# A second expert layer by quarters with seven block products in place of eight, in a fused attention and expert kernel

## The chip, the cores and the metric

One core of a Trainium2 chip runs the whole program. The metric is device microseconds of one execution, as a median of several runs on one chip. Executions of one kernel mostly lie within about 0.3% of each other, so a difference of 1 or 2 us is not read from a total here, but from the traces.

Engine names are those of the profile: PE is TensorE, PEld its weight loads, DVE VectorE, ACT ScalarE, POOL GpSimd, SP SyncE. L432 is line 432 of the kernel that the profile is of; line numbers move from one kernel to the next. The granted clock is the share of its full clock that TensorE was given, as the trace records it.

## The reference

```python
# q, k, v: (8 batches, 8 heads, 576, 64); 4 experts; w1: (4, 512, 1024), w2: (4, 1024, 512)
k_p, v_p = k and v averaged over groups of 8 positions        # 72 keys and values
attn = softmax(q @ k_p.T / 8);  x = attn @ v_p                 # 4608 tokens of 512
p = domain_probs / (domain_probs.sum(-1) + 1e-9)
for e in range(4):
    h = relu(x @ w1[e])
    out += p[:, e] * (h @ w2[e])          # the second expert layer
```

## The kernel before

Tokens come in nine chunks of 512: eight from one batch each, and one of what the batches leave over. Four experts make 36 pairs of chunk and expert. In step s, TensorE does the first layer of pair s and, in turns with it, the second layer of pair s-1. Pieces of the next chunk's attention are strewn into the four steps of a chunk. The order on each engine is fixed by the program. A bank is a part of PSUM, the memory that takes TensorE's results; an evacuation is the instruction of VectorE (DVE) or ScalarE (ACT) that reads a result out of its bank; a fold is VectorE's averaging of one batch's keys or values over groups of 8. The remainder is the ninth chunk.

```python
psum_a = tile_pool(bufs=2)   # attention: two pairs of banks
psum_h = tile_pool(bufs=2)   # first layer: two banks
psum_o = tile_pool(bufs=2)   # second layer: two banks
...
def down(c, e, r):                      # second layer, 128 tokens
    o_ps = psum_o.tile([P, DM], F32)
    for fc in range(8):
        matmul(o_ps, lhsT=H_sb[:, fc, r*P:(r+1)*P], rhs=w2_bf[:, e, fc, :])   # 128x512
    if e == 0: nc.scalar.activation(out=acc[:, r, :], in_=o_ps, func=Copy, scale=prob)
    else:      nc.vector.scalar_tensor_tensor(acc[:, r, :] = o_ps * prob + acc[:, r, :])
...
def scores(b, pair):                    # 64 rows: pairs, which start 3 to 4 ns apart in the trace
    matmul(sc_ps[0:72, r2, hh], lhsT=kpT[lo:lo+64, h, 0:72], rhs=qT[lo:lo+64, h])   # x4
    nc.scalar.activation(out=expT, in_=sc_ps[0:72], func=Exp)
...
for i in range(4):                      # one step
    up(c, e, two of the eight fc); slot(); down(previous pair, i); slot()
```

The softmax here doesn't subtract the row's maximum and nothing guards it: scores larger than these inputs give would overflow.

## Time and profile before

| | before |
|---|---|
| median of runs | 555.96 us |
| PE busy, granted clock | 543.2 us (98%), 0.999 |
| DVE busy, ACT busy | 28%, 42% |
| start to start, 128x512 matmul with its own weights | 216 ns |

The first view is the page of the kernel before: busy time and count of instructions of each engine, and the chain that ended last.

```profile
PE 543.2 (98%) x2975; PEld 251.5 (45%) x2975; DVE 154.0 (28%) x254; ACT 233.3 (42%) x375; POOL 40.3 (7%) x59
...
PE 90%; DMA 8%; POOL 1%; DVE 0%; issue 0%; ACT 0%; POOLq 0%
```

TensorE is the bound, and the chain of waits runs through it. The groups of the same page say what it does. Columns: line, engine, operation, output and inputs, sizes, count; then busy time and mean ns of one; then idle time before.

```profile
L432 PE MATMUL o_ps<-w_bf,H_sb 128*128 128x512 bf16 x1152 | 271.7, 379 | 0.0
L443 DVE SCALAR_TENSOR_TENSOR acc<-o_ps,p_all,acc 128x512 f32<-128x512 f32 x108 | 81.1, 751 | 331.6 <-PE o_ps L432 331.2
```

The mean of 379 ns is the duration that the trace gives one matmul (its end is modelled); as one starts every 216 ns, the records overlap. What a matmul costs is read from start to start. The next view is the timeline of PE (start us, duration us, engine, line, group):

```profile
32.90 1.89 PE L432 MATMUL o_ps<-w_bf,H_sb 128*128 128x512 bf16 x8
34.63 1.89 PE L422 MATMUL h_ps<-xT,w_bf 128*128 128x512 bf16 x8
...
219.61 0.41 PE L243 MATMUL sc_ps<-qT,kpT 64*72 64x256 bf16 x4
219.95 1.90 PE L432 MATMUL o_ps<-w_bf,H_sb 128*128 128x512 bf16 x8
```

Eight matmuls of 512 columns take 34.63 - 32.90 = 1.73 us, 216 ns each. A step has 64 of them, 13.82 us, and a step without attention takes 13.81 us in the trace: nothing else is left in it. In the first steps TensorE waits for a load, in the same view (in brackets the idle time before the first of the group, and what ended it):

```profile
47.76 0.40 PE L228 MATMUL qt_ps<-ident,q_sb 128*128 128x128 bf16 x4 [0.88 <-DMA q_sb<-in_q_dram]
```

### The profile page before, as it was taken

What the parts mean: (1) busy time and instruction counts of PE and PEld (TensorE: products, weight loads), DVE (VectorE), ACT (ScalarE), POOL (GpSimd) and SP (SyncE); (2) the same over time, 40 slices, a digit from 0 to 9 for tenths busy, and PEclk for the clock granted to TensorE, in tenths of its full rate; (3) what the DMA queues carried; (4) which work ended last, traced back from release to release, by engine and by line L of the source; (5) the groups of instructions that cost most, each with busy time, mean ns of one, the idle gap of its engine ahead of it and who ended that gap; (6) DMA issues with size and microseconds to landing.
All of it is one profiled execution on the core that took longest, in us unless ns stands there. A gap on an engine that the chain in (4) does not pass through costs nothing.

```text
span 553.9 us, 7058 instructions
## 1 busy us (share of the span) xinstructions
PE 543.2 (98%) x2975; PEld 251.5 (45%) x2975; DVE 154.0 (28%) x254; ACT 233.3 (42%) x375; POOL 40.3 (7%) x59
## 2 busy tenths in 40 slices
PE   8899999999999999999999999999999999999996
PEld 4654444444444444444444444444444444444442
DVE  2404435033502342132403250335023201220122
ACT  1653533633364335533463346333643344334330
POOL 6410301000020002000200020000000000000000
PEclk9999999999999999999999999999999999999999
DMA  9999996900591139302851178004001110011003
GB/s 125 209 208 206 200 91 141 132 20 19 108 142 16 28 80 156 49 20 39 161 66 28 11 153 120 20 19 108 20 11 29 54 33 0 2 47 39 0 1 76
DMA packets 73407, 41.37 MB, mean 75 GB/s; under 512 B 44688, under 2 KB 67216, under 8 KB 73376
## 3 DMA queue, kind: packets, MB, share of 16 engines
q0 software_dynamic: 32032, 22.63, 28.2%
q1 hardware_dynamic: 41344, 18.29, 15.3%
q8 instruction: 23, 0.38, 0.3%
q14 instruction: 8, 0.07, 0.1%
HBM read 45.16 MB, written 9.44 MB: 99 GB/s over the span
## 4 chain that ended last, share of the span: by engine, by line
PE 90%; DMA 8%; POOL 1%; DVE 0%; issue 0%; ACT 0%; POOLq 0%
PE o_ps L432 44%; PE h_ps L422 42%; DMA q_sb<-in_q_dram 5%; DMA w_bf<-in_moe_w_dram 2%; PE sc_ps L243 2%; PE c_ps L268 1%; DMA x_rem<-x_tok 0%; POOL kraw L84 0%; PE scr_ps L306 0%; POOL q_sb L92 0%; POOL vraw L84 0%; DVE acc L443 0%; PE c_ps L322 0%; PE qt_ps L228 0%; ACT expT L246 0%
## 5 line engine op out<-in xcount | busy, mean ns | idle before, releaser
L426 ACT ACTIVATE H_sb<-h_ps 128x512 bf16<-128x512 f32 (+1 forms) x296 | 173.2, 585 | 249.6 <-PE h_ps L422 247.7
L432 PE MATMUL o_ps<-w_bf,H_sb 128*128 128x512 bf16 x1152 | 271.7, 379 | 0.0
L422 PE MATMUL h_ps<-xT,w_bf 128*128 128x512 bf16 (+1 forms) x1056 | 242.8, 373 | 0.8 <-ACT xT L286 0.4
L443 DVE SCALAR_TENSOR_TENSOR acc<-o_ps,p_all,acc 128x512 f32<-128x512 f32 x108 | 81.1, 751 | 331.6 <-PE o_ps L432 331.2
L422 PEld LDWEIGHTS <-w_bf 128*128 128x128 bf16 x1184 | 113.0, 98 | 130.1 <-issue 4.9
L432 PEld LDWEIGHTS <-H_sb 128*128 128x128 bf16 x1152 | 110.2, 98 | 131.1 <-issue 2.7
L440 ACT ACTIVATE acc<-o_ps,p_all 128x512 f32<-128x512 f32 x36 | 24.7, 687 | 39.4 <-PE o_ps L432 39.4
L246 ACT ACTIVATE expT<-sc_ps 72x1024 bf16<-72x1024 f32 x32 | 32.0, 1011 | 3.6 <-PE sc_ps L243 3.6
L422 PE MATMUL h_ps<-x_rem,w_bf 128*128 128x512 bf16 x128 | 30.2, 379 | 0.2 <-DMA x_rem<-x_tok 0.2
L257 DVE TENSOR_TENSOR x_tok<-c_ps,inv 128x512 bf16<-128x512 f32 x36 | 24.9, 692 | 1.2
L398 POOL COPY gate<-kpT 1x1 bf16<-1x1 bf16 x6 | 2.1, 348 | 264.8 <-DMA kpT<-kp_97 144.8
L268 PEld LDWEIGHTS <-expT 72*128 72x128 bf16 x256 | 12.4, 98 | 7.8 <-ACT expT L246 0.9
L256 DVE RECIPROCAL inv<-c_ps 128x8 f32<-128x8 f32 x36 | 7.3, 203 | 26.2 <-PE c_ps L268 17.2
L157 DVE TENSOR_TENSOR kraw<-kraw 72x2048 bf16<-72x2048 bf16 x7 | 8.5, 1212 | 20.7 <-DMA kraw<-in_k_dram 20.7
L243 PE MATMUL sc_ps<-qT,kpT 64*72 64x256 bf16 x128 | 13.1, 282 | 0.6 <-ACT expT L246 0.5
L205 PE MATMUL w_ps<-zeros 128*128 128x512 bf16 x31 | 10.8, 488 | 1.2 <-DVE zeros L459 1.2
L243 PEld LDWEIGHTS <-kpT 64*72 64x72 bf16 x128 | 4.8, 107 | 12.9 <-issue 12.3
L157 DVE TENSOR_TENSOR vraw<-vraw 72x2048 bf16<-72x2048 bf16 x7 | 8.5, 1210 | 0.0
L92 POOL DMA_DIRECT2D q_sb<-in_q_dram x9 | 7.8, 870 | 2.0 <-issue 2.0
L84 POOL DMA_DIRECT2D kraw<-in_k_dram x9 | 7.6, 843 | 2.4 <-PE xt_ps L285 2.0
L84 POOL DMA_DIRECT2D vraw<-in_v_dram x9 | 7.3, 810 | 1.5 <-issue 0.5
L102 POOL DMA_DIRECT2D q_rem<-in_q_dram x8 | 5.6, 698 | 8.4 <-DMA w_bf<-in_moe_w_dram 8.4
(56 smaller groups left out, 88.0 us busy)
## 6 DMA issues: line engine op xcount, KB each, us to landing
out_dram<-acc SPq DMA_DIRECT2D x32, 256.0 KB, 2.4
w_bf<-in_moe_w_dram POOLq DMA_DIRECT2D x7, 1024.0 KB, 23.1
kraw<-in_k_dram POOLq DMA_DIRECT2D x7, 576.0 KB, 11.2
vraw<-in_v_dram POOLq DMA_DIRECT2D x7, 576.0 KB, 13.7
q_sb<-in_q_dram POOLq DMA_DIRECT2D x7, 512.0 KB, 7.0
w_bf<-in_moe_w_dram POOLq DMA_DIRECT2D x2, 512.0 KB, 12.6
out_dram<-acc SPq DMA_DIRECT2D x8, 128.0 KB, 2.3
kraw<-in_k_dram POOLq DMA_DIRECT2D x2, 288.0 KB, 5.3
```

The costliest lines, as they stand in the source:

```text
L84: nc.gpsimd.dma_start(out=raw[:, hs], in_=src[b, hs].rearrange("h (j r) d -> j h r d", r=POOL))
L157: nc.vector.tensor_add(out=raw[:, hs, 0:4, :], in0=raw[:, hs, 0:4, :], in1=raw[:, hs, 4:8, :])
L205: nc.tensor.matmul(w_ps[:], lhsT=zeros[:, 0:P], rhs=zeros[:])
L243: nc.tensor.matmul(sc_ps[0:SP, r2, hh], lhsT=kpT[lo:lo + D, h, 0:SP], rhs=qT[lo:lo + D, h])
L246: nc.scalar.activation(out=expT[:, 2 * pair:2 * pair + 2].rearrange("j h a b t -> j b (h a) t"), in_=sc_ps[0:SP].rearrange("j b h a t -> j ...
L257: nc.vector.tensor_tensor(out=x_tok[:], in0=c[:, :, :, 0:D], in1=inv[:].unsqueeze(3).to_broadcast([P, 2, NPAIR, D]), op=ALU.mult,)
L268: nc.tensor.matmul(c_ps[:, h // NPAIR, at:at + D + 1], lhsT=expT[:, h, r // 2, r % 2, :], rhs=vp[:, h, :],)
L422: nc.tensor.matmul(out_ps, lhsT=w1_bf[:, e, kc, fc * P:(fc + 1) * P], rhs=xT[:, kc, at], start=(kc == 0), stop=(kc == KC - 1),)
L426: nc.scalar.activation(out=H_sb[:, fc, at], in_=out_ps, func=ACT.Relu)
L432: nc.tensor.matmul(o_ps[:], lhsT=H_sb[:, fc, r * P:(r + 1) * P], rhs=w2_bf[:, e, fc, :], start=(fc == 0), stop=(fc == FCH - 1),)
L440: nc.scalar.activation(out=accs[c][:, r, :], in_=o_ps[:], func=ACT.Copy, scale=prob)
L443: nc.vector.scalar_tensor_tensor(out=dst, in0=o_ps[:], scalar=prob, in1=dst, op0=ALU.mult, op1=ALU.add,)
```

## The change

A block product of 2 by 2 quarters needs eight products of quarters. A known scheme (Winograd's form of Strassen's) gets by with seven, for eight sums of quarters. Here the quarters of the hidden layer are `a11..a22` (halves of the tokens by halves of the hidden columns), those of the weights `b11..b22`. Sums of weights are made once for each expert, sums of hidden quarters in each step, all in bf16 on VectorE. The scheme shares partial results: a bank is read by VectorE as soon as one product is in it, goes on growing by the next product, and is read again for another quarter of the output.

```diff
-    psum_a bufs=2; psum_o bufs=2; accpool bufs=2; hpool bufs=3
+    psum_a bufs=1; psum_o: four banks o0..o3; one acc; hpool bufs=2
...
+    def weight_sums(e):                       # once for each expert, in place for b12
+        t0 = b12 - b11;  b12 = b22 - b12;  t1 = b22 - t0;  t2 = b21 - t1
+    early_sum: S3 = a11 - a21;  hidden_sums: S1 = a21 + a22, S2 = S1 - a11;  last_sum: S4 = a12 - S2
...
+        chain, grows, lhs, rhs, row, col, first = [
+            ("o0", 0, a11, b11, 0, 0, True),  ("o2", 0, a12, b21, 0, 0, False),
+            ("o0", 1, S2, t1, 0, 1, True),    ("o2", 0, S1, t0, 1, 1, True),
+            ("o0", 1, S3, b12, 1, 1, False),  ("o2", 1, S4, b22, 0, 1, False),
+            ("o0", 1, a22, t2, 1, 0, True)][step]
+        for j in range(2):                    # two banks of 128 tokens x 256 columns
+            for i in range(4):
+                matmul(o_ps, lhsT=lhs[:, i, j*P:(j+1)*P], rhs=rhs[:, i, :],
+                       start=(not grows and i == 0), ...)
+            if e == 0 and first: nc.scalar.activation(out=dst, in_=o_ps, func=Copy, scale=prob)
+            else: nc.vector.scalar_tensor_tensor(dst = o_ps * prob + dst)
...
-                lhsT=kpT[lo:lo + D, h, 0:SP]
+                lhsT=key_columns(b, h, lo)    # 128 columns, 56 of them not used
...
+            if (s, i) in ((0, 6), (1, 5), (3, 0), (3, 6)): weight_sums(...)   # experts 1 to 4
```

A step then has 32 matmuls of 512 columns for the first layer and 56 of 256 for the second. The first batch's attention borrows product banks, since they are free at that time.

More of the change, by code (lines that the diff above doesn't have):

```diff
@@ L51 @@
     rawpool = ctx.enter_context(tc.tile_pool(name="rawpool", bufs=1))
-    apool = ctx.enter_context(tc.tile_pool(name="apool", bufs=2))
+    apool = ctx.enter_context(tc.tile_pool(name="apool", bufs=1))
     xpool = ctx.enter_context(tc.tile_pool(name="xpool", bufs=2))
     npool = ctx.enter_context(tc.tile_pool(name="npool", bufs=2))
-    hpool = ctx.enter_context(tc.tile_pool(name="hpool", bufs=3))
-    accpool = ctx.enter_context(tc.tile_pool(name="accpool", bufs=2))
-    psum_a = ctx.enter_context(tc.tile_pool(name="psum_a", bufs=2, space=bass.MemoryType.PSUM))
+    hpool = ctx.enter_context(tc.tile_pool(name="hpool", bufs=2))
+    spool = ctx.enter_context(tc.tile_pool(name="spool", bufs=1))
+    psum_a = ctx.enter_context(tc.tile_pool(name="psum_a", bufs=1, space=bass.MemoryType.PSUM))
     psum_h = ctx.enter_context(tc.tile_pool(name="psum_h", bufs=2, space=bass.MemoryType.PSUM))
-    psum_o = ctx.enter_context(tc.tile_pool(name="psum_o", bufs=2, space=bass.MemoryType.PSUM))
+    psum_o = ctx.enter_context(tc.tile_pool(name="psum_o", bufs=1, space=bass.MemoryType.PSUM))
     w1_bf = wpool.tile([P, E, KC, F], BF16, name="w1_bf")
     w2_bf = wpool.tile([P, E, FCH, DM], BF16, name="w2_bf")
+    wt_bf = wpool.tile([P, E, 3, FCH // 2, DM // 2], BF16, name="wt_bf")
+    acc = const.tile([P, NR, DM], F32, name="acc")
     x_rem = const.tile([P, NPAIR, NT], BF16, name="x_rem")
@@ L70 @@
     kps = [const.tile([SPT, H, 2, D], BF16, name=f"kp{i}") for i in range(2)]
+    kpTs = [const.tile([P, H + 1, SPT], BF16, name=f"kpT{i}") for i in range(3)]
     vps = [const.tile([SP, H, D + 1], BF16, name=f"vp{i}") for i in range(3)]
@@ L154, with spare_bank @@
     state = {}
+    turns = [0]
+    def spare_bank():
+        turns[0] += 1
+        return psum_o.tile([P, NT], F32, tag=f"o{turns[0] % 4}", name="spare")
     def fold(raw, hs):
@@ L170, in keys @@
     def keys(b, hs):
-        if hs.start == 0:
-            state[("kpT", b)] = apool.tile([P, H, SPT], BF16, name="kpT", bufs=3)
+        state[("kpT", b)] = kpTs[b % 3]
         if b >= BUSY:
             nc.sync.dma_start_transpose(
-                out=state[("kpT", b)][:], in_=kps[b % 2][:].rearrange("j h a d -> j (h a d)")
+                out=state[("kpT", b)][:, 0:H], in_=kps[b % 2][:].rearrange("j h a d -> j (h a d)")
             )
             return
-        kpt_ps = psum_o.tile([P, H, SP], BF16, tag="o_ps", name="kpt_ps")
+        kpt_ps = one_bank(b).bitcast(BF16)[:, 0:H * SP].rearrange("p (h j) -> p h j", j=SP)
         for h in range(hs.start, hs.stop):
@@ L223, in queries @@
             return
-        pool, tag = (psum_o, "o_ps") if b == 0 else (psum_a, "a")
-        qt_ps = pool.tile([P, 2, 2, P], BF16, tag=tag, name="qt_ps")
+        qt_ps = one_bank(b).bitcast(BF16)[:, 0:4 * P].rearrange("p (h a t) -> p h a t", h=2, a=2)
         for hh in range(2):
@@ L230, in queries, with key_columns @@
                 )
-        nc.vector.tensor_copy(out=state[("qT", b)][:, 2 * pair:2 * pair + 2], in_=qt_ps[:])
+        nc.vector.tensor_copy(out=state[("qT", b)][:, 2 * pair:2 * pair + 2], in_=qt_ps)
+    def key_columns(b, h, lo):
+        return state[("kpT", b)][:].rearrange("p h j -> p (h j)")[lo:lo + D, h * SPT:h * SPT + P]
     def scores(b, pair):
-        kpT, qT = state[("kpT", b)], state[("qT", b)]
+        qT = state[("qT", b)]
         if pair == 0:
@@ L237, in scores @@
         expT = state[("expT", b)]
-        sc_ps = psum_a.tile([P, 2, 2, 2, P], F32, tag="a", name="sc_ps")
+        banks = two_banks(b == 0 and pair % 2)
         for hh in range(2):
@@ L243, in scores, with one_bank, two_banks, whole @@
                 nc.tensor.matmul(
-                    sc_ps[0:SP, r2, hh], lhsT=kpT[lo:lo + D, h, 0:SP], rhs=qT[lo:lo + D, h]
-                )
-        nc.scalar.activation(
-            out=expT[:, 2 * pair:2 * pair + 2].rearrange("j h a b t -> j b (h a) t"),
-            in_=sc_ps[0:SP].rearrange("j b h a t -> j b (h a) t"),
-            func=ACT.Exp, scale=EXP_SCALE,
-        )
-    def divide(c_ps, x_tok):
-        c = c_ps[:, :, 0:NPAIR * (D + 1)].rearrange("p a (h d) -> p a h d", d=D + 1)
-        inv = npool.tile([P, 2, NPAIR], F32, name="inv")
-        nc.vector.reciprocal(out=inv[:], in_=c[:, :, :, D])
-        nc.vector.tensor_tensor(
-            out=x_tok[:], in0=c[:, :, :, 0:D],
-            in1=inv[:].unsqueeze(3).to_broadcast([P, 2, NPAIR, D]), op=ALU.mult,
-        )
+                    banks[r2][:, hh * 2 * P:(hh + 1) * 2 * P],
+                    lhsT=key_columns(b, h, lo), rhs=qT[lo:lo + D, h],
+                )
+        exp_out = expT[:, 2 * pair:2 * pair + 2].rearrange("j h a b t -> j b (h a) t")
+        for sc, r2 in whole(banks):
+            nc.scalar.activation(
+                out=exp_out[:, r2], in_=sc[0:SP].rearrange("j b (g t) -> j b g t", t=P),
+                func=ACT.Exp, scale=EXP_SCALE,
+            )
+    def one_bank(b):
+        return spare_bank()[:] if b == 0 else two_banks(False)[0]
+    def two_banks(spare):
+        if spare:
+            return [spare_bank()[:], spare_bank()[:]]
+        t = psum_a.tile([P, 2, NT], F32, tag="a", name="a_ps")
+        return [t[:, 0], t[:, 1], t]
+    def whole(banks):
+        if len(banks) == 3:
+            return [(banks[2][:], slice(0, 2))]
+        return [(banks[i].unsqueeze(1), slice(i, i + 1)) for i in range(2)]
+    def divide(banks, x_tok):
+        for ps, hs in whole(banks):
+            n = hs.stop - hs.start
+            c = ps[:, :, 0:NPAIR * (D + 1)].rearrange("p a (h d) -> p a h d", d=D + 1)
+            inv = npool.tile([P, 2, NPAIR], F32, name="inv")
+            nc.vector.reciprocal(out=inv[:, 0:n], in_=c[:, :, :, D])
+            nc.vector.tensor_tensor(
+                out=x_tok[:, hs], in0=c[:, :, :, 0:D],
+                in1=inv[:, 0:n].unsqueeze(3).to_broadcast([P, n, NPAIR, D]), op=ALU.mult,
+            )
     def context(b, r):
@@ L264, in context @@
         x_tok = npool.tile([P, 2, NPAIR, D], BF16, name="x_tok", bufs=4)
-        c_ps = psum_a.tile([P, 2, NT], F32, tag="a", name="c_ps")
+        banks = two_banks(b == 0 and r % 2)
         for h in range(H):
@@ L268, in context @@
             nc.tensor.matmul(
-                c_ps[:, h // NPAIR, at:at + D + 1],
+                banks[h // NPAIR][:, at:at + D + 1],
                 lhsT=expT[:, h, r // 2, r % 2, :], rhs=vp[:, h, :],
             )
-        divide(c_ps, x_tok)
+        divide(banks, x_tok)
         state[("x", b, r)] = x_tok
@@ L282, in turn @@
             return
-        xt_ps = psum_o.tile([P, KC, P], BF16, tag="o_ps", name="xt_ps")
+        xt_ps = spare_bank()[:].bitcast(BF16)[:, 0:KC * P].rearrange("p (k t) -> p k t", t=P)
         for kc in range(KC):
             nc.tensor.transpose(xt_ps[:, kc, :], x_tok[:, kc * P:(kc + 1) * P], ident[:])
-        nc.scalar.copy(out=dst, in_=xt_ps[:])
+        nc.scalar.copy(out=dst, in_=xt_ps)
     def rem_queries(i):
@@ L301, in rem_scores @@
         for bb in range(2):
-            kpT = state[("kpT", 2 * i + bb)]
             for pair in range(NPAIR):
@@ L306, in rem_scores @@
                     nc.tensor.matmul(
-                        scr_ps[0:SP, hh, bb, pair, :],
-                        lhsT=kpT[lo:lo + D, 2 * pair + hh, 0:SP],
+                        scr_ps[:, hh, bb, pair, :],
+                        lhsT=key_columns(2 * i + bb, 2 * pair + hh, lo),
                         rhs=qTr[lo:lo + D, pair, bb, :],
@@ L317, in rem_context @@
         x_tok = npool.tile([P, 2, NPAIR, D], BF16, name="x_tok", bufs=4)
-        c_ps = psum_a.tile([P, 2, NT], F32, tag="a", name="c_ps")
+        banks = two_banks(False)
         for h in range(H):
@@ L322, in rem_context @@
                 nc.tensor.matmul(
-                    c_ps[bb * REM:(bb + 1) * REM, h // NPAIR, at:at + D + 1],
+                    banks[h // NPAIR][bb * REM:(bb + 1) * REM, at:at + D + 1],
                     lhsT=expTr[:, h % 2, bb, h // 2, :], rhs=vps[(2 * i + bb) % 3][:, h, :],
                 )
-        divide(c_ps, x_tok)
+        divide(banks, x_tok)
         state[("xr", i)] = x_tok
@@ L410 @@
     hidden = {}
-    accs = {}
     def up(c, e, fcs, at=slice(0, NT)):
@@ L426, in up @@
             nc.scalar.activation(out=H_sb[:, fc, at], in_=out_ps, func=ACT.Relu)
-    def down(c, e, r):
-        H_sb = hidden[(c, e)]
-        o_ps = psum_o.tile([P, DM], F32, name="o_ps")
-        for fc in range(FCH):
-            nc.tensor.matmul(
-                o_ps[:], lhsT=H_sb[:, fc, r * P:(r + 1) * P], rhs=w2_bf[:, e, fc, :],
-                start=(fc == 0), stop=(fc == FCH - 1),
-            )
-        prob = p_all[:, c * NR + r, e:e + 1]
-        if e == 0:
-            if r == 0:
-                accs[c] = accpool.tile([P, NR, DM], F32, name="acc")
-            nc.scalar.activation(out=accs[c][:, r, :], in_=o_ps[:], func=ACT.Copy, scale=prob)
-            return
-        dst = accs[c][:, r, :]
-        nc.vector.scalar_tensor_tensor(
-            out=dst, in0=o_ps[:], scalar=prob, in1=dst,
-            op0=ALU.mult, op1=ALU.add,
-        )
-        if e < E - 1:
-            return
+    HF, HN, HD = FCH // 2, NT // 2, DM // 2
@@ new lines, with combine @@
+    LO, HI = slice(0, HF), slice(HF, FCH)
+    BANKS = 2
+    def combine(dst, a, op, b):
+        nc.vector.tensor_tensor(out=dst, in0=a, in1=b, op=op)
+    def weight_sums(e):
+        w, t = w2_bf[:, e], wt_bf[:, e]
+        b11, b12 = w[:, LO, 0:HD], w[:, LO, HD:DM]
+        b21, b22 = w[:, HI, 0:HD], w[:, HI, HD:DM]
+        combine(t[:, 0], b12, ALU.subtract, b11)
+        combine(b12, b22, ALU.subtract, b12)
+        combine(t[:, 1], b22, ALU.subtract, t[:, 0])
+        combine(t[:, 2], b21, ALU.subtract, t[:, 1])
@@ new lines, in quarters, with early_sum, hidden_sums @@
+    def quarters(c, e):
+        H_sb = hidden[(c, e)]
+        return [H_sb[:, LO, 0:HN], H_sb[:, HI, 0:HN], H_sb[:, LO, HN:NT], H_sb[:, HI, HN:NT]]
+    def early_sum(c, e):
+        a11, a12, a21, a22 = quarters(c, e)
+        state[("S3", c, e)] = spool.tile([P, HF, HN], BF16, name="S3", bufs=2)
+        combine(state[("S3", c, e)][:], a11, ALU.subtract, a21)
+    def hidden_sums(c, e):
+        a11, a12, a21, a22 = quarters(c, e)
+        s1 = spool.tile([P, HF, HN], BF16, name="S1")
+        s2 = spool.tile([P, HF, HN], BF16, name="S2")
+        combine(s1[:], a21, ALU.add, a22)
+        combine(s2[:], s1[:], ALU.subtract, a11)
+        state["S1"], state["S2"] = s1, s2
@@ new lines, in last_sum, with down @@
+    def last_sum(c, e):
+        a11, a12, a21, a22 = quarters(c, e)
+        state["S4"] = spool.tile([P, HF, HN], BF16, name="S4")
+        combine(state["S4"][:], a12, ALU.subtract, state["S2"][:])
+    def down(c, e, step):
+        w, t = w2_bf[:, e], wt_bf[:, e]
+        a11, a12, a21, a22 = quarters(c, e)
+        if step == 0:
+            hidden_sums(c, e)
+        chain, grows, lhs, rhs, row, col, first = [
+            lambda: ("o0", 0, a11, w[:, LO, 0:HD], 0, 0, True),
+            lambda: ("o2", 0, a12, w[:, HI, 0:HD], 0, 0, False),
+            lambda: ("o0", 1, state["S2"], t[:, 1], 0, 1, True),
+            lambda: ("o2", 0, state["S1"], t[:, 0], 1, 1, True),
+            lambda: ("o0", 1, state[("S3", c, e)], w[:, LO, HD:DM], 1, 1, False),
+            lambda: ("o2", 1, state["S4"], w[:, HI, HD:DM], 0, 1, False),
+            lambda: ("o0", 1, a22, t[:, 2], 1, 0, True),
+        ][step]()
+        for j in range(BANKS):
+            tag = f"o{int(chain[1]) + j}"
+            if not grows:
+                state[tag] = psum_o.tile([P, NT], F32, tag=tag, name="o_ps")
+            o_ps = state[tag][:, 0:HD]
+            for i in range(HF):
+                nc.tensor.matmul(
+                    o_ps, lhsT=lhs[:, i, j * P:(j + 1) * P], rhs=rhs[:, i, :],
+                    start=(not grows and i == 0), stop=(i == HF - 1),
+                    skip_group_check=True,
+                )
+            r = row * BANKS + j
+            prob = p_all[:, c * NR + r, e:e + 1]
+            dst = acc[:, r, col * HD:(col + 1) * HD]
+            if e == 0 and first:
+                nc.scalar.activation(out=dst, in_=o_ps, func=ACT.Copy, scale=prob)
+            else:
+                nc.vector.scalar_tensor_tensor(
+                    out=dst, in0=o_ps, scalar=prob, in1=dst, op0=ALU.mult, op1=ALU.add,
+                )
+            if e == E - 1 and step in (5, 6):
+                store(c, r)
+        if step == 1:
+            last_sum(c, e)
@@ L449, in down, with store @@
+    def store(c, r):
         if c < B:
             rows = out[c * S:c * S + NT, :].rearrange("(p r) d -> p r d", r=NR)
-            nc.sync.dma_start(out=rows[:, r, :], in_=dst)
+            nc.sync.dma_start(out=rows[:, r, :], in_=acc[:, r, :])
         else:
@@ L454, in down @@
                 at = (2 * r + bb) * S + NT
-                nc.sync.dma_start(out=out[at:at + REM, :], in_=dst[bb * REM:(bb + 1) * REM])
+                nc.sync.dma_start(out=out[at:at + REM, :],
+                                  in_=acc[bb * REM:(bb + 1) * REM, r, :])
     nc.vector.memset(zeros[:], 0.0)
@@ L461 @@
         nc.vector.memset(vp[:, :, D:D + 1], float(POOL))
+    for kpT in kpTs:
+        nc.vector.memset(kpT[:], 0.0)
     for kp in kps:
@@ L465 @@
     steps = [(c, e) for c in range(NCH) for e in range(E)]
-    SLOTS = E * NR * 2
+    SLOTS = E * FCH
     ENG = mybir.EngineType
@@ L512 @@
                     due = -late * per_slot
-            for i in range(NR):
+            for i in range(FCH):
                 if 0 < s < len(steps):
-                    n = FCH // NR
-                    up(c, e, range(i * n, (i + 1) * n))
-                slot()
-                if s > 0:
+                    up(c, e, (i,))
+                if s > 0 and i < 7:
                     down(*steps[s - 1], i)
                 slot()
+                if s < len(steps) and i == HF:
+                    early_sum(c, e)
+                if (s, i) in ((0, 6), (1, 5), (3, 0), (3, 6)):
+                    weight_sums({(0, 6): 0, (1, 5): 1, (3, 0): 2, (3, 6): 3}[(s, i)])
 _INS = ['q', 'k', 'v', 'moe_domain_probs', 'moe_w1', 'moe_w2']
```

## The prediction

> **What bounds the kernel now.** TensorE. The page gives PE 543.2 of 553.9 us (98%) at a granted clock of 0.999, against DVE 154.0 (28%) and ACT 233.3 (42%); the chain that ended last is 90% PE. Start to start in the trace, a 128x512 matmul takes 216 ns, and the 128x256 ones of the first batch's first layer, each with its own 128x128 weight load, 109 ns. The Trainium skill ("TensorE: Matmul & The Clock Gate", Back-to-back issue gap) gives N/2.4+2.5 ns, 215.8 and 109.2; the trace agrees.
>
> **Products.** 36 steps x 32 matmuls of 512 columns become 36 x 56 of 256: 1152 x 216 = 248.8 us becomes 2016 x 109 = 219.7. Gain 29 us, all on the chain.
>
> **Scores.** Keys are read as 128 columns in place of 72. The same page (Weight-path perf modes) says that the fast weight load needs 128 weights. In the trace a scores piece costs 93 ns before it and 342 inside it, where two pairs at 109 would do; context pieces with 128-column weights show no such wait. About 0.2 us x 30: gain 5 us (estimate).
>
> **Added to VectorE.** A sum of 1024 bf16 elements took 687 ns; 144 make 99 us. Weight sums: 16, 11 us. Evacuations: 512 columns took 751 ns; 256 I estimate at 0.49 us. Of 14 per step, 8 of the first expert's are on ACT: 432 on DVE, 210 us in place of 81. DVE goes to about 395 us, 73-77%; about 10 us of a 13 us step for experts 2 to 4, plus 0.9 us per context and 5.1 us of folds per batch. ACT rises to about 245 us.
>
> **What comes back onto the chain (estimates).** A growing bank must be read before its next product, about 2.6 us later, so an evacuation may lag by some 2 us.
> - Folds (2.7 and 2.3 us) stand in the last expert's step, where DVE is full: S2 and the bank of product 0 come about 1 us late per batch: +5 us.
> - Weight sums of experts 3 and 4 (5.5 us) in one early step: DVE 16 us in a 14.5 us step: +2.
> - At about 46 us the queue of loads limits: PE waited 0.9 us for q_sb; it will wait more: +1.
> - Tail: the last step runs at DVE's pace, about 10 us instead of 7: +3.
> - Accumulator without a second buffer (ACT waits for the store, 2.4 us to landing), single attention banks, contexts in full steps: +2.
>
> Sum: 556 - 29 - 5 + 13 = 535 us, ratio 0.962. Range 525 to 547 us. Chances: faster by over 2% 0.86, within 2% 0.12, slower 0.02.
>
> **Right or wrong in the profile.** Groups: 2016 matmuls of 256 columns on o_ps, 109 ns start to start inside a product. DVE 370-420 us; H_sb sums 0.69 us, evacuations 0.46-0.52. PE idle by releaser: o_ps waiting for acc (bank not yet read) or S tiles, mostly in last experts' steps, 5-10 us in all. Wait before sc_ps gone. Timeline: a chunk of four steps takes about 56.4 us now, 53.5 after.
>
> **What would make it wrong.** DVE slower than estimated (evacuations near 0.6 us, or sums slowed by strides): it would set the pace of experts 2 to 4 and most of the gain would go. 256-column matmuls over 109 ns among semaphore waits. Scores not gaining. In the other direction: if DVE's queue absorbs the folds, 525-528 us.

## The result, and the profile after

The kernel after has a median of 538.88 us (536.75 to 539.54, four runs), the kernel before 556.11 us on the same chip. The ratio is 0.9686, 95% interval 0.9657 to 0.9715. Ratios in this document are the mean time of one kernel's fast runs over that of the other's of the same rounds, so not quite the ratio of the medians quoted.

The page and the groups of the kernel after, in the columns of those shown of before (the two lines of L525 are two of the groups that hold the 2016 products):

```profile
PE 516.9 (96%) x3839; PEld 335.5 (62%) x3839; DVE 365.2 (68%) x745; ACT 238.3 (44%) x413; POOL 41.6 (8%) x59
...
PE 85%; DMA 8%; DVE 4%; POOL 1%; ACT 1%; issue 0%; DVEq 0%; POOLq 0%
...
L525 PE MATMUL o_ps<-w_bf,H_sb 128*128 128x256 bf16 x576 | 74.5, 273 | 0.0
L525 PE MATMUL o_ps<-wt_bf,H_sb 128*128 128x256 bf16 x288 | 37.3, 273 | 0.0
L536 DVE SCALAR_TENSOR_TENSOR acc<-o_ps,p_all,acc 128x256 f32<-128x256 f32 x432 | 194.1, 481 | 96.0 <-PE o_ps L525 78.6
```

DVE went from 154 to 365 us, PE fell by only 26 us of busy time, and VectorE now has 4% of the chain. The timeline of PE after gives the cost of a product:

```profile
37.67 1.04 PE L525 MATMUL o_ps<-wt_bf,S_501 128*128 128x256 bf16 x8
...
38.54 1.03 PE L452 MATMUL h_ps<-xT,w_bf 128*128 128x512 bf16 x4
```

That is 0.87 us for eight, 109 ns each, weight loads hidden. A step should take 32 x 216 + 56 x 109 ns = 13.02 us. The view of windows shows one step of the middle without attention on TensorE, before and after (window, its length, then busy time and count of instructions of PE, PEld, DVE, ACT and POOL, clock, DMA share, GB/s):

```profile
196.10:209.90 13.80, 13.80 (x66) 6.26 (x65) 5.57 (x8) 4.78 (x8) 0.00 (x0) 1.00 0.49 116
```

```profile
195.10:208.12 13.02, 13.02 (x90) 8.62 (x88) 10.04 (x20) 4.78 (x8) 0.00 (x0) 1.00 0.20 38
```

TensorE is busy for the whole of the window in both: the saving of 0.8 us per step arrives in full. Each step from 4 to 34 saves 0.74 to 0.91 us, except step 31 (0.20), but the two ends do not. The table is worked out from both traces; a step is counted from its first ReLU (ACT's instruction on a first-layer result), about 1.1 us after its first matmul.

| stretch | before, us | after, us | difference | wanted at 0.81 per step |
|---|---|---|---|---|
| to step 1 | 32.24 | 31.95 | -0.3 | 0 |
| step 1 | 13.81 | 13.78 | 0.0 | -0.8 |
| step 2 | 19.11 | 21.57 | +2.5 | -0.8 |
| step 3 | 14.88 | 18.19 | +3.3 | -0.8 |
| steps 4 to 34 | 449.52 | 425.19 | -24.3 | -25.1 |
| from step 35 to the end | 24.38 | 26.82 | +2.4 | -1.6 |
| sum | 553.94 | 537.50 | -16.4 | -29.1 |

So 12.7 us of the wanted gain are missing: 8.2 in the first three steps, 4.1 at the end, 0.7 in the middle (0.6 of it in step 31, where TensorE waits for the remainder tokens' transposed copy and gets there earlier than before), less 0.3 at the start.

The timeline of the kernel after shows the waits of the first steps. In brackets is the idle time before the first of a group, and what ended it.

```profile
35.92 1.05 PE L525 MATMUL o_ps<-wt_bf,S_502 128*128 128x256 bf16 x8 [0.46 <-DVE S_502 L471]
...
48.29 0.40 PE L237 MATMUL a_ps<-ident,q_sb 128*128 128x128 bf16 x4 [1.77 <-DMA q_sb<-in_q_dram]
...
50.86 0.38 PE L237 MATMUL a_ps<-ident,q_sb 128*128 128x128 bf16 x4 [0.43 <-DVE qT L240]
...
52.57 0.38 PE L237 MATMUL a_ps<-ident,q_sb 128*128 128x128 bf16 x4 [1.33 <-DVE qT L240]
...
65.93 0.42 PE L300 MATMUL a_ps<-vp_105,expT 72*128 72x65 bf16 x8 [1.11 <-ACT expT L262]
...
71.40 1.03 PE L525 MATMUL o_ps<-wt_bf,S_861 128*128 128x256 bf16 x8 [0.46 <-DVE wt_bf L471]
...
74.36 0.43 PE L300 MATMUL a_ps<-vp_105,expT 72*128 72x65 bf16 x8 [1.92 <-DVE x_tok L289]
```

The line at 35.92 is step 1: S2 stands in VectorE's queue behind the weight sums of the first expert. In the trace these sums had themselves waited 1.93 us for the DMA of their weights (`w_bf`), so this loss is the load's as well as VectorE's. Step 2 has the load of `q_sb` and then three waits for a copy, or for the exponential, of the piece of attention before. Step 3 has two waits for VectorE, and right after them the clock falls, as the view of windows says (the eighth number is the granted clock):

```profile
69.90:74.80 4.90, 2.52 (x27) 1.46 (x24) 4.80 (x11) 0.60 (x1) 0.00 (x0) 1.00 1.77 128
74.80:78.70 3.90, 3.90 (x16) 2.02 (x15) 2.06 (x5) 0.60 (x1) 0.00 (x0) 0.56 1.31 96
```

In the first window VectorE is busy for 4.80 of 4.90 us and TensorE for 2.52; in the second TensorE is at half clock for most of the time. The trace records half clock from 75.19 us for 3.41 us.

### The profile page after: what moved, and what is told of

Same layout as the page of the kernel before. It is cut to its first block, busy times and chain, and to the rows that moved or that the text cites. A ratio compares the mean times of both kernels' runs of the same rounds, so it can differ in the third digit from the quotient of the medians.

```text
span 537.5 us, 9393 instructions
## 1 busy us (share of the span) xinstructions
PE 516.9 (96%) x3839; PEld 335.5 (62%) x3839; DVE 365.2 (68%) x745; ACT 238.3 (44%) x413; POOL 41.6 (8%) x59
## 4 chain that ended last, share of the span: by engine, by line
PE 85%; DMA 8%; DVE 4%; POOL 1%; ACT 1%; issue 0%; DVEq 0%; POOLq 0%
PE h_ps L452 43%; PE o_ps L525 38%; DMA kraw<-in_k_dram 4%; DMA w_bf<-in_moe_w_dram 3%; PE a_ps L256 2%; PE a_ps L300 1%; DVE acc L536 1%; DMA x_rem<-x_tok 0%; ACT expT L262 0%; DVE wt_bf L471 0%; POOL q_sb L97 0%; PE a_ps L353 0%; POOL kraw L89 0%; POOL vraw L89 0%; DVE x_tok L289 0%
## 5 line engine op out<-in xcount | busy, mean ns | idle before, releaser
L452 PE MATMUL h_ps<-xT,w_bf 128*128 128x512 bf16 (+1 forms) x1056 | 260.4, 374 | 0.7 <-ACT xT L318 0.4
L536 DVE SCALAR_TENSOR_TENSOR acc<-o_ps,p_all,acc 128x256 f32<-128x256 f32 x432 | 194.1, 481 | 96.0 <-PE o_ps L525 78.6
L525 PEld LDWEIGHTS <-H_sb 128*128 128x128 bf16 x864 | 84.5, 98 | 32.5 <-DMA w_bf<-in_moe_w_dram 0.4
L525 PE MATMUL o_ps<-w_bf,H_sb 128*128 128x256 bf16 x576 | 74.5, 273 | 0.0
L525 PE MATMUL o_ps<-wt_bf,H_sb 128*128 128x256 bf16 x288 | 37.3, 273 | 0.0
L262 ACT ACTIVATE expT<-a_ps 72x1024 bf16<-72x1024 f32 x30 | 30.5, 1017 | 13.7 <-PE a_ps L256 13.7
L534 ACT ACTIVATE acc<-o_ps,p_all 128x256 f32<-128x256 f32 x72 | 31.3, 472 | 3.9 <-DMA out_dram<-acc 3.4
L289 DVE TENSOR_TENSOR x_tok<-a_ps,inv 128x512 bf16<-128x512 f32 x34 | 23.5, 691 | 1.2
L288 DVE RECIPROCAL inv<-a_ps 128x8 f32<-128x8 f32 x34 | 6.7, 198 | 3.5 <-PE a_ps L300 3.1
L168 DVE TENSOR_TENSOR kraw<-kraw 72x2048 bf16<-72x2048 bf16 x7 | 8.5, 1212 | 0.3 <-DMA kraw<-in_k_dram 0.3
L300 PE MATMUL a_ps<-vp_105,expT 72*128 72x65 bf16 x96 | 5.1, 194 | 3.0 <-DVE x_tok L289 1.9
```

The source lines that it names most:

```text
L168: nc.vector.tensor_add(out=raw[:, hs, 0:4, :], in0=raw[:, hs, 0:4, :], in1=raw[:, hs, 4:8, :])
L262: nc.scalar.activation(out=exp_out[:, r2], in_=sc[0:SP].rearrange("j b (g t) -> j b g t", t=P), func=ACT.Exp, scale=EXP_SCALE,)
L289: nc.vector.tensor_tensor(out=x_tok[:, hs], in0=c[:, :, :, 0:D], in1=inv[:, 0:n].unsqueeze(3).to_broadcast([P, n, NPAIR, D]), op=ALU.mult,)
L300: nc.tensor.matmul(banks[h // NPAIR][:, at:at + D + 1], lhsT=expT[:, h, r // 2, r % 2, :], rhs=vp[:, h, :],)
L452: nc.tensor.matmul(out_ps, lhsT=w1_bf[:, e, kc, fc * P:(fc + 1) * P], rhs=xT[:, kc, at], start=(kc == 0), stop=(kc == KC - 1),)
L525: nc.tensor.matmul(o_ps, lhsT=lhs[:, i, j * P:(j + 1) * P], rhs=rhs[:, i, :], start=(not grows and i == 0), stop=(i == HF - 1), skip_group ...
```

## The experiments

Theory A said that VectorE's new work makes attention late in the first steps, and that the tail runs at VectorE's pace. The rivals were the single pair of attention banks, and the loads. Twelve kernels were run. Each compares with the kernel before on its own chip; spans and steps are of the profiled run. Expectations count a step from its first matmul, so that their "84.4" is 85.5 in the count of the table above.

### The base again

> The changed kernel unaltered, as the base of this call. All theories: 537 to 540 us, ratio to the kernel before about 0.969; step 4 of the second layer starts near 84 us.

No edit. Measured: 538.08 us median (536.92 to 538.96), ratio 0.9672; step 3 took 18.20 us, step 2 21.95.

### The first four steps by eight products

```diff
+    def plain(c, e): return c == 0
+    # plain pairs: 128x512 products of w2 itself into banks o0..o3, evacuated as before
-    weight_sums at (0, 6), (1, 5), (3, 0), (3, 6)
+    weight_sums at (2, 1), (3, 1), (4, 1), (5, 1)
```

> The first four steps use the eight products again, and the weight sums move into steps 2 to 5. Theory A (the first steps lose because VectorE, with quarter sums, twice as many evacuations and weight sums, answers attention late): the start of step 4 goes back from 84.4 to about 79 us and the total to about 533.5. Theory B (one pair of attention banks, or loads, and not VectorE's work): the start of step 4 stays at 82 us or later, since four steps each get 0.8 us longer on TensorE; total 539 or more.

Measured: 537.68 us (537.22 to 539.85), ratio 0.9675. Neither theory had the total; the start of step 4, 82.0 us from its first matmul, is where B put it. Step 3 fell from 18.20 to 15.33 us, as A has it, but step 2 stayed at 22.34, though it had no sums of the hidden layer and 4 evacuations of 512 columns in place of 14 of 256. Steps 1, 2 and 4 together took 1.6 us longer, which uses up over half of what step 3 gave. So VectorE counts in step 3. For step 2 this run alone does not decide, because the edit also moved the first expert's weight sums, 2.75 us of VectorE, into that step; the runs with two pairs of banks and with one pair in the kernel before decide it.

### The last step by eight products

```diff
+    def plain(c, e): return (c, e) == (NCH - 1, E - 1)
+    w2_last: a copy of b12 of the last expert, made before the weight sums write over it
```

> The very last step uses eight products, with one quarter of the weights kept aside. If the tail is paced by VectorE (two sums, then fourteen evacuations of 0.48 us and a sum), the span from the start of step 35 falls from 27.9 to about 24.7 us, total about 535.7. If the tail is stores and latency, no change within 1 us.

Measured: 536.99 us (536.46 to 538.25), ratio 0.9657. In the trace the stretch from step 35 to the end fell from 26.79 to 23.82 us, by 3.0 us, as expected from VectorE's pace. The medians show 1.1 us of it, but the runs spread by 2 us, and in the profiled one step 1, which the edit does not touch, was 1.2 us longer than in the base. How the tail goes with seven products is seen in the chain of waits of the kernel after (start us, length us, what):

```profile
523.41 0.70 DVE S_6092 L471
...
524.14 0.69 DVE S_6093 L471
524.83 0.41 DVE acc L536
...
525.28 0.61 PE o_ps L525 x4
...
525.93 0.47 DVE acc L536
526.40 0.60 DVE S_6120 L471
527.00 0.41 DVE acc L536
...
527.45 1.05 PE o_ps L525 x8
528.50 0.13 DVE acc L536
...
528.88 1.65 DVE acc L536 x4
```

The chain goes through two sums and a first evacuation before the third product may start, and after that it is nearly all VectorE.

### Both ends by eight products

> Both of the former. If the two losses are separate, the gains add: about 530 us, ratio about 0.953.

The edit is the sum of the last two. Measured: 534.76 us (534.03 to 536.55), ratio 0.9619; the span was 532.7, 4.5 us under the base's 537.2. The gains add in the trace (1.4 + 3.0); the expected 530 took too large a gain for the first steps.

### Without the weight sums of experts 3 and 4

```diff
-                if (s, i) in ((0, 6), (1, 5), (3, 0), (3, 6)):
+                if (s, i) in ((0, 6), (1, 5)):
+    nc.vector.memset(wt_bf[:, 2:4], 0.0)      # at the start; the result is wrong on purpose
```

> The weight sums of experts 3 and 4 are left out (their tile is set to zero at the start; wrong on purpose). If these 5.5 us of VectorE's queue set the loss of the step in which they stand, it falls from 18.2 to about 15 us and the total by 2.5 to 4 us. If the single pair of attention banks sets it, less than 1 us.

Measured: 535.64 us (534.52 to 537.22), ratio 0.9616, against 0.9672 to 0.9686 for the base. Step 3 took 14.00 us: 4.2 us less than with the sums, and 0.9 less than in the kernel before. The view of windows, of the kernel after and then of this one, shows the stretch of step 3:

```profile
66.00:84.20 18.20, 15.82 (x120) 10.06 (x120) 14.33 (x31) 4.18 (x7) 0.00 (x0) 0.91 1.11 107
```

```profile
66.00:80.00 14.00, 13.96 (x119) 9.46 (x119) 11.75 (x26) 4.18 (x7) 0.00 (x0) 1.00 1.50 143
```

TensorE is busy nearly throughout and the half clock is gone too: the trace records none before TensorE's last work, only in the last 4.6 us of the span. So the weight sums make the whole loss of step 3, about 0.5 + 1.9 us of waits and up to 1.7 us of the clock (half of 3.41).

### The first steps with two pairs of attention banks

```diff
+    # as both_plain; for the second batch's attention two_banks() gives psum_a and (o2, o3) in turn
-    tag=f"o{r}"
+    tag=f"o{r % 2 if c == 0 else r}"          # plain products of the first chunk in two banks
```

> As both_plain, but the products of the first four steps alternate between two banks, as in the kernel before, and the attention of that stretch gets the other two as a second pair. If the one pair of attention banks holds up step 2 (transposes waiting for the copy of the one before, 1.2 us, context for the exponential, 1.3 us, scores 0.3 us twice), step 2 falls from 21.5 to 19 or 20 us and the total to about 532. If only the wait for the load of q_sb counts there, step 2 stays within 0.5 us.

Measured: 532.00 us (531.63 to 534.65), ratio 0.9561, interval 0.9527 to 0.9595, the lowest of all. Step 2 took 20.96 us, against 21.46 in both_plain, but the wait for `q_sb` happened to be longer: 2.88 us in place of 1.54. Without that wait, step 2 fell from 19.9 to 18.1 us. Step 3 fell from 15.33 to 14.60. In both_plain the timeline has these waits in step 2:

```profile
47.39 0.40 PE L238 MATMUL a_ps<-ident,q_sb 128*128 128x128 bf16 x4 [1.54 <-DMA q_sb<-in_q_dram]
...
51.63 0.38 PE L238 MATMUL a_ps<-ident,q_sb 128*128 128x128 bf16 x4 [1.03 <-DVE qT L241]
...
66.02 0.42 PE L301 MATMUL a_ps<-vp,expT 72*128 72x65 bf16 x8 [1.11 <-ACT expT L263]
```

With two pairs the waits for copies and the exponential shrink from 2.4 to 0.6 us there; the load remains (columns: engine and group that waited, what it waited for; us in total, times, longest):

```profile
PE spare L238 <- DMA q_sb<-in_q_dram: 2.9, 1, 2.9
```

So the single bank pair is some 2 us of step 2, and the load is the rest. A count that leaves the load out agrees. From the first use of `q_sb` to the start of step 4 (first ReLU) the traces take 37.20 us in the kernel after and 37.21 in its repeat, 35.34 both in first_plain and in both_plain, 32.79 here, and 32.28 in the kernel before.

### One pair of attention banks in the kernel before

```diff
-    psum_a = tile_pool(name="psum_a", bufs=2)
+    psum_a = tile_pool(name="psum_a", bufs=1)
```

> The kernel before with one pair of attention banks in place of two, nothing else. If the bank pair alone makes the first steps late, +4 to +6 us, in the steps from 45 to 79 us. If it takes a busy VectorE too, under +2 us.

Measured: 563.00 us (561.44 to 564.47), ratio 1.0105. The loss is not where either theory looked for it: 5.7 us fall before step 1, in the first batch's attention, and 10.2 us of that stretch ran at half clock (18.75 to 28.99 us in the trace; the kernel before has none there). Steps 2 and 3 took 0.4 us more than before, together; but they started 5.7 us later, so that the load of `q_sb` was in time, and waits of 1.03 us for a copy and 1.11 us for the exponential stand in its place. So these waits come from one pair of banks without any of VectorE's new work. It suggests that the change was right to lend product banks to the first batch, and shows that bank waits and load waits hide one another.

### The loads in another order

```diff
         load_w1(2)
-        load_w2(1)
         attention_first()
         load_k(1); load_q(1)
+        load_w2(1)                            # on top of both_plain_two_pairs
```

> As both_plain_two_pairs, with the second batch's keys and queries loaded ahead of the second expert's second-layer weights. If the order of loads is what is left of the loss in step 2 (TensorE waited 1.7 to 3 us for q_sb there), the wait goes, the weights come in time for step 2 or up to 1 us late, and the total falls by 1 to 3 us, to about 530. If the loads' bandwidth as a whole sets it, the wait only moves to the weights and the total stays at 532.

Measured: 532.92 us (532.05 to 535.46, five runs), ratio 0.9592, interval 0.9569 to 0.9616: no gain, and not told apart from both_plain_two_pairs, whose interval it meets. The wait moved to the weights, as the second theory has it:

```profile
PE o_ps L570 <- DMA w_bf<-in_moe_w_dram: 1.2, 1, 1.2
```

Step 2 fell to 19.28 us and step 3 rose to 15.21; step 4 started at the same time within 0.3 us. In this stretch the loads as a whole set the time, as far as this run shows, and not their order.

### Scores with 72 key columns again

```diff
-    h * SPT:h * SPT + P
+    h * SPT:h * SPT + SP                      # and outputs on 72 partitions
```

> Scores with 72 key columns again, all else as changed. The prediction's step (128 columns bring the fast weight load, 0.17 us a piece and more): about +5 us. Rival (the waits of 0.09 us before and after a scores piece come from matmuls on 64 of the 128 rows and stay at 128 columns): +0.5 us at most, gaps 309 and 202 ns in both.

Measured: 539.65 us (537.93 to 540.71), ratio 0.9681, no difference from the base. Two timelines, of this kernel and of the kernel after:

```profile
106.31 1.04 PE L525 MATMUL o_ps<-w_bf,S 128*128 128x256 bf16 x8
107.28 0.41 PE L256 MATMUL a_ps<-qT,kpT 64*72 64x256 bf16 x4
107.62 1.04 PE L452 MATMUL h_ps<-xT,w_bf 128*128 128x512 bf16 x4
```

```profile
108.39 1.04 PE L525 MATMUL o_ps<-w_bf,S_1236 128*128 128x256 bf16 x8
109.36 0.39 PE L256 MATMUL a_ps<-qT,kpT_103 64*128 64x256 bf16 x4
```

In both, the scores start 0.97 us after a group of eight products that takes 0.87: a wait of 0.1 us at either width. Start to start, the last product to the scores takes 202 ns with 72 columns and 205 with 128, the last scores to the next matmul 202 in both; only inside the piece is there a gain, 117 ns in place of 134 between its two pairs.

### Scores on all 128 rows

```diff
-    lhsT=key_columns(b, h, lo), rhs=qT[lo:lo + D, h]
+    lhsT=both halves of the keys, rhs=qT[:, h]     # adds two scores: not what the reference asks
```

> Scores matmuls on all 128 rows (both copies of the keys against both halves of the queries; the result is wrong on purpose). If the waits come from the half array, they go: o_ps to scores 109 ns in place of 205, scores to h_ps 109 in place of 202, but the four matmuls no longer run in pairs, so a piece costs 436 in place of about 420 ns and the total is the same within 1 us. If the waits come from semaphores or banks, the gaps of 205 and 202 stay and the total grows by about 6 us.

Measured: 539.65 us (539.30 to 541.16), ratio 0.9691. (The output still passed the comparison; why is not shown, and that is no reason to use it.) The gaps are gone:

```profile
106.44 1.04 PE L525 MATMUL o_ps<-w_bf,S 128*128 128x256 bf16 x8
107.31 0.60 PE L256 MATMUL a_ps<-qT,kpT 128*128 128x256 bf16 x4
107.75 1.03 PE L452 MATMUL h_ps<-xT,w_bf 128*128 128x512 bf16 x4
```

The scores start 0.87 us after the products, without a wait, and take 4 x 109 ns. So the waits belong to the change between whole and half arrays, not to the number of weights, the banks or the semaphores, which were the same here.

### More work for VectorE in the middle

```diff
             hidden_sums(c, e)
+            for _ in range(2 if 2 <= c <= 6 else 0):    # and 4
+                combine(spare_sum[:], a11, ALU.add, a22)
```

> Two more VectorE sums of 0.69 us at the head of the queue of every step of five middle chunks (20 steps), results unused. If the folds of a batch stand at the edge, as the prediction had it, each chunk loses 1 us or more: +5 us or more. If VectorE's queue has the 3 us of slack per step that busy time shows, under 1 us.

> Four more such sums (2.75 us). VectorE's work of a step reaches 12.8 to 13.6 us where TensorE needs 13.0 to 14.3, so VectorE should set the pace of the last expert's steps at least. By busy time alone about +0.6 us a chunk, +3 us; if the waits of banks bite first, 2 to 3 us a chunk, +10 to +15 us.

Two sums (1.4 us) cost nothing: 539.54 us, ratio 0.9684, and every step of the five chunks took the same time as in the base to 0.02 us, the steps with the folds too. Four sums (2.75 us) made it 554.87 us (552.54 to 555.31), ratio 0.9951: nearly the whole gain. The 20 steps with sums grew by 16.3 us together, 0.3 to 1.1 us each, where the rule by busy time gave 3 and the rule by waits for banks 10 to 15. The wait is that for a bank that VectorE has not read yet:

```profile
PE o_ps L528 <- DVE acc L539: 13.6, 17, 1.0
```

So each of these steps of the kernel after has between 1.4 and 2.75 us to spare on VectorE, for work at the head of its queue. In one of them (197.60 to 211.75 us, grown by 1.13 us) VectorE was then busy for 13.13 of 14.15 us: here the engine set the pace below full load, since its results were wanted in time for a bank.

## Why the prediction was right or wrong

The total was right: 535 us forecast with a range of 525 to 547, 538.88 measured. The mechanism of the gain was right as well. But of the terms, two were wrong by 5 us each and cancelled; that the total came out so near is luck.

| term of the prediction | forecast, us | measured, us | from |
|---|---|---|---|
| products, "216 becomes 109" | -29 | -29.1 due, -24.3 of 25.1 seen in steps 4 to 34 | step table |
| scores at 128 columns | -5 | -0.3 (12 ns x 28 pieces) | keys72, traces |
| folds in the last expert's step | +5 | 0 | middle steps, dve_plus2 |
| weight sums | +2 | +4.2 in step 3 (no_late_sums), and 0.4 to 0.8 in step 1, partly the load's | no_late_sums, both traces of the kernel after |
| load of q_sb | +1 | +0.9 (1.77 against 0.88); +1.3 in the repeat (2.16) | timelines |
| tail | +3 | +4.1 | step table; last_plain: 3.0 come back |
| single buffers and banks | +2 | about 2 in step 2 | both_plain_two_pairs |
| wait for a transposed copy in step 31 | none | +0.6 | step traces |

**Products.** 2016 matmuls of 256 columns at 109 ns. The forecast took that from 64 matmuls of the start of the trace, and it agrees with the formula that the Trainium skill ("TensorE: Matmul & The Clock Gate", Back-to-back issue gap) gives for an isolated matmul at full clock: 256/2.4 + 2.5 = 109.2 ns.

**Scores: the step that failed** is "context pieces with 128-column weights show no such wait", read as a proof that the number of weights makes the wait. Context pieces differ from scores in two things: 128 columns, and more than 64 rows. The trace of before already held the counter-example: the first batch's sums of keys and values on TensorE (`s_ps`, L189) have 72 rows and only 72 columns of weights, and at full clock they start 216 and 226 ns after a 512-column matmul, a wait of 10 ns at most, and run 108 to 114 ns apart. The Trainium skill has the sentence that the forecast overlooked ("TensorEngine Tiling (Array Packing)", Key Properties): changing the tiling mode drains the engine. The full_rows run agrees: with whole arrays the 96 ns before and the 93 ns after (205 and 202 less 109) are gone. The fast weight load that the prediction cited may be at work inside the piece (117 for 134 ns), where it is worth 17 ns.

**Folds.** The step that failed is the hand count of VectorE's queue, "S2 and the bank of product 0 come about 1 us late". No step with folds lost anything, and another 1.4 us in the queue was borne. The sizes of the instructions were right (evacuations 0.481 us for 0.49, sums 0.68 to 0.69 for 0.687, as the skill's "VectorE: DVE Perf Modes", The perf-mode tier table, suggests for bf16: 1224 ns for 2048 elements, 1212 here); the error lay in adding up when each would be wanted.

**First steps.** Named rightly, sized too small. What the prediction missed in step 3 is that a delay of VectorE comes back twice: through the single attention bank pair (TensorE's context piece waits 1.9 us for `x_tok`), and through the clock, which stood at half for 3.41 us afterwards. It put the banks under "+2" without saying that they would bite where attention is packed densest, in the second batch's pieces, at 19 pieces in 14 slots, where later chunks have 29 slots.

**Tail.** As forecast, about 1 us larger. Accumulator without a second buffer: ACT waited for stores eight times, 3.4 us in all, but no wait of TensorE follows from it. VectorE was forecast at about 395 us, and the durations of its instructions in the trace add up to 395.7; the page's busy time of 365.2 us is less because instructions that follow each other closely overlap in the records (two evacuations of 0.48 us show as 0.87 us together) and it counts the overlap once. Three of the signs that the prediction named did not come: the wait before the scores stayed (96 ns), TensorE's waits for unread banks and sums in the last experts' steps (forecast 5 to 10 us) are absent from the middle, and a chunk of four steps takes 59.1 us before and 55.9 after (steps 12 to 15), not 56.4 and 53.5; its saving of 3.2 us is near the 2.9 forecast.

**Why the half clock comes in step 3.** The 14 traces bear on this together, though no run tests it alone. All recorded changes of clock within a trace lie a multiple of 3.41 us apart. Cut into stretches on that grid, the traces show half clock after each stretch at full clock in which TensorE was busy for under 44% of the time, and after none over 45%; at 44 to 45% it went either way. In the kernel after, the stretch before the half clock (71.78 to 75.19 us) was busy for 1.49 of 3.41 us, and in none of the eight such cases with TensorE's work still to come did a single gap in the stretch exceed 1.93 us. The wait of 2.88 us in both_plain_two_pairs fell across two stretches, which were busy for 61% and 54%. So the sum of waits in a stretch counts, and where its borders fall.

What stays open: how far the best version could still go in step 2, where the loads limit.

**A better version.** With eight products in the first four steps and in the last, two pairs of attention banks at the start, and seven products in between, the kernel takes 532.00 us (ratio 0.9561), less than the 538.88 us (0.9686) of the kernel after, whose interval (0.9657 to 0.9715) does not meet it.

## What to carry to other kernels

A scheme that trades matrix work for sums pays where the engine of the sums has slack at that very time: here the steady steps kept nearly all of the gain, and the first and last steps, where nothing else fills TensorE's wait, gave back more than they saved, so a mixture is better than either. Measure the slack by adding work (two sums free, four sums fatal) rather than by busy time. Before a wait is put down to one property of an instruction, look for a second group that has only one of the properties.

## What the Trainium skill lacked or had wrong

- "TensorEngine Tiling (Array Packing)", Key Properties, says that a change of tiling mode drains the engine, but gives no cost. Here it was 96 ns before and 93 ns after a piece of 64-row scores, and 93 to 97 ns after or before pieces of 64 weights' columns.
- "TensorE: Matmul & The Clock Gate", Back-to-back issue gap, gives a sustained 131 ns for 512 columns in a stream of weight load and matmul pairs. Here such streams ran at 216 ns, and at 109 ns for 256 columns, the figures of its formula for the isolated case.
- The same page, HAM oscillation, gives as its rule no idle gaps of over some 3.4 us; its next section adds that frequent small gaps can do it too, but not how much idle time it takes. Here half clock (for 3.41 us, which fits its window of 3413 ns) followed waits of 0.5 and 1.9 us in a stretch of that length where TensorE was busy for 1.49 us, and came in each of the seven profiles that had them; a single wait of 2.9 us in both_plain_two_pairs brought none. In the 14 traces the border lay at 44 to 45% busy in such a stretch, and not at a stretch wholly idle.
- No page gives a time for `scalar_tensor_tensor` from a PSUM bank with an f32 accumulator: 751 ns for 512 columns, 481 for 256.
